# Matmuls of one array split grouped in a slot, tails loaded by batch, weights loaded later: a fused attention and channel-mix kernel

## The chip, the cores and the metric

The kernel runs on one core of one Trainium2 chip. The metric is the device time of one execution in microseconds (us), and medians of several executions are quoted. TensorE does the matmuls, VectorE and ScalarE work element by element, GpSimd casts and masks, and SyncE issues most DMA transfers. In the profile these are PE (its weight loads PEld), DVE, ACT, POOL and SP (SPq where issuing is meant). PEclk is the share of full speed that TensorE's clock was granted.

## The reference

Attention with a forget gate gives x, and a channel mix follows (the code is shortened). Batch is 8, heads 8, sequence 576, head size 64; the mix goes from 512 to 1024 features and back.

```python
def _attn_ref(q, k, v, f):
    scores = np.matmul(q, k.transpose(0, 1, 3, 2)) / np.sqrt(D)
    cum = np.cumsum(np.log(np.clip(f, 0.0001, 1.0)), axis=-1)
    decay = cum[:, :, :, None] - cum[:, :, None, :]
    scores = np.where(causal, -1e9, scores + decay)
    attn = np.exp(scores - np.max(scores, axis=-1, keepdims=True))
    attn = attn / (np.sum(attn, axis=-1, keepdims=True) + 1e-09)
    return np.matmul(attn, v)

def _moe_ref(x, mu_k, mu_r, w_k, w_v, w_r):
    x_prev = ...                              # x one token earlier, 0 first
    xk = mu_k * x + (1.0 - mu_k) * x_prev     # xr the same with mu_r
    k = np.maximum(xk @ w_k, 0.0)
    return (1.0 / (1.0 + np.exp(-(xr @ w_r)))) * (k * k @ w_v)
```

## The kernel before

Two heads of a batch are a pair; there are 32 pairs, four to a batch. The main loop goes through slots. In slot s the scores and exponentials of pair s are made in four pieces, q and k of pair s+1 are transposed (`tp`, then a copy to `qkT`), and the denominators of pair s-1 are summed. After a lag of 6 slots the numerators of pair s-6 (`values`) are multiplied by the reciprocals of their denominators, which gives `x`; `shift` makes `xk` and `xr` from it. Matmuls of the channel mix (`kp`, `rp`, `vp`) are kept in a queue, and `fill` takes some of them between the other steps. The loop, with loads, casts and the conditions for its ends cut:

```python
    LAG = 6
    for s in range(NP + LAG + 1):
        ...
        scores(s, 0); mask(s, 0)
        fill(gap)
        transposes(s + 1)
        fill(gap)
        scores(s, 1); mask(s, 1); mask(s, 2)
        fill(gap)
        denominators(s - 1)
        if s % PRW == 0:                  # PRW is 4, the pairs of a batch
            norm(s // PRW - 1)
        if s % PRW == LAG % PRW and s >= PRW + LAG:
            queue_mix((s - LAG) // PRW - 1)
        fill(gap)
        scores(s, 2)
        fill(gap)
        values(av, 0)                     # av = s - LAG
        fill(gap)
        scores(s, 3); mask(s, 3)
        fill(gap)
        values(av, 1)
        shift(av)
        fill(gap)
```

`norm` takes the reciprocals of a batch's denominators. They have to lie along the rows of a tile of 128 partitions, so they go out to DRAM (`scr`) and come back repeated over 64 partitions (`rb`), one tile to a pair:

```python
        scr = drp.tile([2, PRW, S], F32, name="scr")
        for half, o, n in ((0, 0, H0), (1, H0, S - H0)):       # H0 is 384
            for hh in range(2):
                r0 = 32 * (2 * half + hh)
                nc.sync.dma_start(out=scr[hh, :, o:o + n], in_=Rf[r0:r0 + PRW, 0:n])
        for p in range(PRW):
            rb = rbp.tile([P, S], F32, name="rb")
            for hh in range(2):
                nc.sync.dma_start(out=rb[hh * D:(hh + 1) * D, :],
                                  in_=scr[hh, p].unsqueeze(0).to_broadcast([D, S]))
            rbs[b * PRW + p] = rb
```

Scores use half of TensorE's rows, numerators half of its columns, denominators four columns, and everything else the full array. Each change from one to another costs about 0.10 us, as the prediction works out.

The softmax here doesn't subtract the row's maximum and nothing guards it: scores larger than these inputs give would overflow.

## Time and profile before

| Quantity | Before | Read from |
|---|---|---|
| Median time | 357.1 us (356.22 to 359.68, 4 runs) | runs beside the changed kernel |
| Span of the profiled run | 356.8 us | page |
| First score | 28.5 us | timeline |
| Slot 10 to slot 30, five batches | 84.80 to 267.40, 182.6 us | timeline, windows |

The slots 10 to 29 are five batches in the steady part. They are the best yardstick here, since each kernel does the same work in five such batches. The view by windows of the kernel before gives them so: stretch, its length, busy us and instructions of five engines, mean granted clock, DMA share, GB/s.

```profile
84.80:267.40 182.60, 177.71 (x1773) 94.81 (x1770) 136.72 (x252) 104.84 (x182) 95.59 (x140) 0.98 0.65 167
```

TensorE had no matmul open for 182.60 - 177.71 = 4.9 us of it, at a clock of 0.98.

### The profile page before, as it was taken

Reading aid. Unit: us, or ns where it says so; the run is one execution under the profiler, and the core shown is the slowest. Engines: PE = TensorE matmul, PEld = TensorE weight load, DVE = VectorE, ACT = ScalarE, POOL = GpSimd, SP = SyncE. Lnnn points to the kernel's source line nnn. Section 1 sums busy time; section 2 is a strip of 40 time slices with the busy share of each in tenths; the row PEclk is TensorE's granted clock in tenths of the full one; section 3 lists DMA queues with packets and bytes.
Section 4 is the critical chain, followed back from the end, with each engine's and each line's share of the span. In section 5 each row is a group of like instructions: output and inputs, shape, how many; then the busy total and the mean of one; then the engine's idle time right before and its main releaser. Section 6 shows DMA issues by size and latency. Waiting matters only on the chain.

```text
span 356.8 us, 7628 instructions
## 1 busy us (share of the span) xinstructions
PE 300.6 (84%) x2853; PEld 163.1 (46%) x2853; DVE 226.1 (63%) x443; ACT 175.6 (49%) x296; POOL 151.2 (42%) x231
## 2 busy tenths in 40 slices
PE   0006889577799999999999999999999978896995
PEld 0003445344445455545454555454545534553562
DVE  3043232397639786968697969685978677786442
ACT  1015667354637475647464756464646521440451
POOL 3003668577245574545555745355555322100000
PEclk9999999686989999999999999999999989999899
DMA  7996663764768576767754765676544315211012
GB/s 131 203 174 139 153 143 127 176 153 130 188 139 200 145 196 143 194 177 193 174 139 167 190 160 141 193 197 162 130 155 108 94 36 165 91 61 59 2 59 88
DMA packets 129029, 50.61 MB, mean 142 GB/s; under 512 B 118049, under 2 KB 119713, under 8 KB 128993
## 3 DMA queue, kind: packets, MB, share of 16 engines
q1 hardware_dynamic: 126896, 47.51, 52.1%
q0 software_dynamic: 2096, 2.62, 4.4%
q8 instruction: 22, 0.36, 0.4%
q14 instruction: 15, 0.11, 0.1%
HBM read 43.14 MB, written 9.58 MB: 148 GB/s over the span
## 4 chain that ended last, share of the span: by engine, by line
PE 53%; SPq 15%; DVE 13%; issue 5%; DMA 5%; ACT 4%; POOL 3%; POOLq 0%; DVEq 0%; ACTq 0%
PE vp L345 14%; PE kp L333 11%; SPq L96 9%; PE rp L345 7%; PE sc L226 6%; PE num L298 4%; PE tp L168 4%; DMA kf<-in_k_dram 4%; SPq L99 4%; PE den L259 3%; ACT a L232 3%; SPq L285 2%; PE vp L349 2%; DVE xk L322 2%; DVE x L304 2%
## 5 line engine op out<-in xcount | busy, mean ns | idle before, releaser
L232 ACT ACTIVATE a<-sc 128x1024 bf16<-128x1024 f32 (+2 forms) x128 | 105.8, 835 | 74.0 <-PE sc L226 70.1
L244 POOL TENSOR_SCALAR_AFFINE_SELECT a<-a 128x256 bf16<-128x256 bf16 (+2 forms) x128 | 62.1, 498 | 124.4 <-ACT a L232 119.8
L333 PE MATMUL kp<-xk,wk_sb 128*128 128x288 bf16 x512 | 76.7, 293 | 7.4 <-DVE xk L322 5.3
L337 ACT ACTIVATE rel<-kp 128x288 bf16<-128x288 f32 x128 | 51.6, 412 | 41.4 <-PE kp L333 27.7
L345 PE MATMUL vp<-wv_sb,relusq 128*128 128x512 bf16 x256 | 61.9, 385 | 2.0 <-DVE x L304 2.0
L333 PEld LDWEIGHTS <-wk_sb 128*128 128x128 bf16 x512 | 46.0, 99 | 26.9 <-issue 11.2
L226 PE MATMUL sc<-qkT 64*128 64x192 bf16 (+4 forms) x512 | 51.0, 282 | 7.8 <-ACT a L232 5.1
L158 POOL TENSOR_TENSOR vw<-vf,wbf 128x640 bf16<-128x640 f32 x32 | 45.5, 1423 | 20.2 <-PE num L298 11.8
L338 DVE TENSOR_TENSOR relusq<-rel 128x288 bf16<-128x288 bf16 x128 | 39.8, 331 | 18.9 <-ACT rel L337 17.6
L366 DVE SCALAR_TENSOR_TENSOR res<-th,vp 128x512 f32<-128x512 f32 x36 | 24.6, 683 | 37.7 <-PE vp L345 21.8
L304 DVE TENSOR_TENSOR x<-num,rb 128x384 bf16<-128x384 f32 x64 | 28.5, 456 | 20.8 <-PE num L298 18.6
L169 DVE COPY qkT<-tp 128x1152 bf16<-128x1152 bf16 x32 | 24.0, 750 | 26.1 <-PE tp L168 26.0
L226 PEld LDWEIGHTS <-qkT 64*128 64x128 bf16 x512 | 21.1, 100 | 42.3 <-issue 40.1
L322 DVE SCALAR_TENSOR_TENSOR xk<-diff,mu_k_sb,x 128x576 bf16<-128x576 bf16 x32 | 39.5, 1236 | 1.1
L359 ACT ACTIVATE th<-rp 128x512 f32<-128x512 f32 x36 | 21.5, 597 | 36.8 <-PE rp L345 33.4
L345 PEld LDWEIGHTS <-relusq 128*128 128x128 bf16 x256 | 23.7, 98 | 29.8 <-issue 3.2
L298 PE MATMUL num<-a,vw 128*64 128x192 bf16 (+4 forms) x512 | 36.3, 269 | 0.0
L345 PE MATMUL rp<-wr_sb,xr 128*128 128x512 bf16 x128 | 34.0, 389 | 0.0
L168 PE MATMUL tp<-ident,qb 128*128 128x128 bf16 (+1 forms) x160 | 19.3, 240 | 13.6 <-DVE qb L153 7.8
L322 DVE SCALAR_TENSOR_TENSOR xr<-diff,mu_r_sb,x 128x576 bf16<-128x576 bf16 x32 | 30.6, 956 | 0.0
L168 PE MATMUL tp<-ident,kb 128*128 128x128 bf16 (+1 forms) x160 | 19.4, 241 | 11.8 <-DVE kb L153 9.2
L298 PEld LDWEIGHTS <-vw 128*64 128x64 bf16 x512 | 22.0, 114 | 14.9 <-issue 11.1
(49 smaller groups left out, 186.7 us busy)
## 6 DMA issues: line engine op xcount, KB each, us to landing
rb<-scr SPq DMA_DIRECT2D x64, 144.0 KB
out_dram<-res SPq DMA_DIRECT2D x36, 256.0 KB
qf<-in_q_dram SPq DMA_DIRECT2D x64, 128.0 KB
kf<-in_k_dram SPq DMA_DIRECT2D x64, 128.0 KB
vf<-in_v_dram SPq DMA_DIRECT2D x64, 128.0 KB
wk_sb<-in_moe_w_k_dram POOLq DMA_DIRECT2D x1, 1024.0 KB, 9.7
qf<-in_q_dram SPq DMA_DIRECT2D x32, 32.0 KB
wv_sb<-in_moe_w_v_dram POOLq DMA_DIRECT2D x1, 1024.0 KB, 18.5
```

What stands on the lines that cost most here:

```text
L158: nc.gpsimd.tensor_tensor(out=vw[Pi % NV], in0=vf[Pi % NV], in1=wbf[:, :, 2 * Pi:2 * Pi + 2].unsqueeze(3).to_broadcast([P, NC, 2, D]), op= ...
L168: nc.tensor.transpose(tp[:, i, c * P:c * P + sz], src[:sz, c, :], ident[:sz, :sz])
L226: nc.tensor.matmul(sc[:, hh, col - off:col - off + n], lhsT=t[lo:lo + D, 1, kb * P:(kb + 1) * P], rhs=t[lo:lo + D, 0, q0:q0 + n], start=Tr ...
L232: nc.scalar.activation(out=a[:, :, off:off + w], in_=sc[:, :, 0:w], func=AF.Exp, scale=SCALE)
L244: nc.gpsimd.affine_select(out=v_, in_=v_, compare_op=ALU.is_ge, fill=0.0, base=0, pattern=pat, channel_multiplier=-1)
L298: nc.tensor.matmul(nm[hh * D:(hh + 1) * D, q0 - o:q0 - o + w], lhsT=t[:, kb, hh, :], rhs=a[:, hh, col:col + w], start=(kb == 0), stop=(kb ...
L304: nc.vector.tensor_tensor(out=xs[Pi % NX][:, 1 + o:1 + o + n], in0=nm[:, 0:n], in1=rbs[Pi][:, o:o + n], op=ALU.mult)
L322: nc.vector.scalar_tensor_tensor(out=dst[:, p, :], in0=diff, scalar=mu[:, p:p + 1], in1=x[:, 0:S], op0=ALU.mult, op1=ALU.add)
L333: nc.tensor.matmul(kp[:, :HB], lhsT=wk_sb[:, db, fb * P:(fb + 1) * P], rhs=xks[b][:, db, hf * HB:(hf + 1) * HB], start=(db == 0), stop=(db ...
L337: nc.scalar.activation(rel, kp[:, :HB], func=AF.Relu)
L338: nc.vector.tensor_mul(rsq[b][:, fb, hf * HB:(hf + 1) * HB], rel, rel)
L345: nc.tensor.matmul(ps, lhsT=tiles[b][:, i, t0:t0 + P], rhs=w[:, i, :], start=(i == 0), stop=(i == n - 1))
```

## The change

Its intent is to take away changes of the array's split (427 before, 185 after, counted in the built order) and to start earlier. It has five parts:

- Scores stand two and two, and the denominators together with both halves of the values, so that matmuls of one split follow each other. `fill` is called three times in a slot, and gates and values of the mix are queued half a batch later.
- The last 64 tokens (the tail) of q, k and v come once a batch, in one transfer each.
- The weights are loaded in slots 1 to 3 instead of at the start, q and k of the first pair come on two queues, and the casts of pair 1 stand behind the chain of f.
- The tails are transposed at full height, which spares two changes of the split for each tensor.
- The reciprocals of four pairs are one tile: one `scr` and four `rb` transfers instead of four and eight. The lag falls from 6 to 5, so the exponentials need six buffers instead of seven; the rows have two tiles of four pairs instead of six of one. `norm` moves to the end of its slot, and the values of the last three pairs come one or two slots earlier.

```diff
-        Rf = R.rearrange("p a b -> p (a b)")
-        scr = drp.tile([2, PRW, S], F32, name="scr")
+        scr = drp.tile([4, 32, H0], F32, name="scr")
+        nc.sync.dma_start(out=scr.rearrange("g r c -> (g r) c"),
+                          in_=R.rearrange("p a b -> p (a b)"))
+        rb = rbp.tile([P, PRW, S], F32, name="rb")
         for half, o, n in ((0, 0, H0), (1, H0, S - H0)):
             for hh in range(2):
-                r0 = 32 * (2 * half + hh)
-                nc.sync.dma_start(out=scr[hh, :, o:o + n], in_=Rf[r0:r0 + PRW, 0:n])
+                nc.sync.dma_start(
+                    out=rb[hh * D:(hh + 1) * D, :, o:o + n],
+                    in_=scr[2 * half + hh, 0:PRW, 0:n].unsqueeze(0).to_broadcast([D, PRW, n]))
 ...
-    LAG = 6
+    LAG = 5
 ...
         if live:
             scores(s, 0)
             mask(s, 0)
-        fill(gap)
 ...
             scores(s, 1)
             mask(s, 1)
             mask(s, 2)
+        fill(1.4)
+        if s + 1 < NP:
+            transposes(s + 1)
 ...
+        fill(1.2)
+        if live:
+            scores(s, 2)
+            scores(s, 3)
+            mask(s, 3)
 ...
         if 0 <= s - 1 < NP:
             denominators(s - 1)
-            if s % PRW == 0:
-                norm(s // PRW - 1)
+        for Pi in avs:
+            values(Pi, 0)
+            values(Pi, 1)
 ...
+        if 0 < s <= NP and s % PRW == 0:
+            norm(s // PRW - 1)
+        for Pi in avs:
 ...
+            shift(Pi)
+        fill(2.5)
```

Cut from this diff, mostly without a mark, are the loads, the tails, the weights, the queue of the mix and removed lines of the old loop.

## The prediction

> **What bounds the kernel now.** I read the page's busy shares and slices first, then the waits, then the timeline of single stretches, because TensorE is busy 84% of the span and an average hides where the other 16% lies. The slices (40 of 8.9 us; digits are tenths):
>
> ```profile
> PE 300.6 (84%) x2853; PEld 163.1 (46%) x2853; DVE 226.1 (63%) x443; ACT 175.6 (49%) x296; POOL 151.2 (42%) x231
> ...
> PE   0006889577799999999999999999999978896995
> ...
> PEclk9999999686989999999999999999999989999899
> DMA  7996663764768576767754765676544315211012
> ```
>
> There are three regimes. For three slices TensorE does nothing while DMA is full; up to slice 11 it has holes and a lowered clock; from then on it is full. In the full part its own stream sets the end. What that stream consists of is read from the timeline (start us, length us, engine, line, operation, count):
>
> ```profile
> 155.10 1.90 PE L345 MATMUL vp<-wv_sb,relusq 128*128 128x512 bf16 x8
> 156.94 0.34 PE L226 MATMUL sc<-qkT 64*128 64x192 bf16 x4
> ...
> 161.45 0.53 PE L168 MATMUL tp<-ident,qb 128*128 128x128 bf16 x5
> 161.91 0.53 PE L168 MATMUL tp<-ident,kb 128*128 128x128 bf16 x5
> ```
> ```profile
> 345.91 1.89 PE L345 MATMUL vp<-wv_sb,relusq 128*128 128x512 bf16 x8
> 347.64 1.03 PE L345 MATMUL rp<-wr_sb,xr 128*128 128x512 bf16 x4
> 348.50 1.89 PE L345 MATMUL vp<-wv_sb,relusq 128*128 128x512 bf16 x8
> ```
>
> The reader should compare starts. Eight vp matmuls before a rp of the same shape take 347.64 - 345.91 = 1.73 us, 216 ns each. The same eight before a sc, which uses half the rows, take 1.84 us. Changing the split of the array costs about 0.10 us. The five transposes confirm it: four at 56 ns and a half-width one at 27 ns are 0.25 us, yet 0.46 us pass, because the 64-row tail switches twice.
>
> The start is a chain of a load and of VectorE's order:
>
> ```profile
> 17.26 0.49 DVE L153 CAST kb<-kf 128x640 bf16<-128x640 f32 x1 [9.51 <-DMA kf<-in_k_dram]
> ...
> 24.64 0.39 DVE L182 TENSOR_SCALAR lf<-lf 64x576 f32<-64x576 f32 x1
> ...
> 28.25 0.55 PE L191 MATMUL wtp<-ident,wrow 64*128 64x64 f32 x3 [9.68 <-ACT wrow L187]
> ```
>
> The first k tile comes at 17.3 us, while 2.5 MB of weights share the DMA engines; the f chain waits behind the casts of pair 1. First score: 28.5 us. Later holes are those of the SyncE queue, which issues without a break:
>
> ```profile
> 62.70 1.09 SPq L96 DMA_DIRECT2D kf<-in_k_dram  x2
> 63.84 0.63 SPq L99 DMA_DIRECT2D kf<-in_k_dram  x1
> 64.56 1.10 SPq L96 DMA_DIRECT2D vf<-in_v_dram  x2
> 65.70 0.61 SPq L99 DMA_DIRECT2D vf<-in_v_dram  x1
> 66.36 1.14 SPq L96 DMA_DIRECT2D qf<-in_q_dram  x2
> ```
>
> One tensor of a pair costs 1.8 us of issuing, q, k and v 5.5 us a slot, against slots of 4.65 to 4.9 us at first. After the 5 us of eight rb issues slots 7, 8 and 9 (sc start to sc start) last 9.4, 6.2 and 7.0 us.
>
> **What the Trainium skill says.** "TensorEngine Tiling (Array Packing)", Tiling Modes, Key Properties: changing the tiling mode, not just the tile, drains TensorE. The trace agrees: 0.10 us. "TensorE: Matmul & The Clock Gate", Back-to-back issue gap, gives N/2.4 + 2.5 ns, so 216 ns at 512 columns; the trace has 216. "Trainium Kernel Development and Optimization", Key Constraints: DMAs of the SP, ACT and POOL queues share the same 16 engines, and a second issuing engine saves only issue time. Here the k loads on ScalarE therefore save issue time, and only the later weights free bandwidth. "SBUF — State Buffer", Who interferes with whom: VectorE operations can be blocked for the length of a GpSimd operation. The trace agrees: xk takes 1.70 us at 160.53 while vw runs from 160.16 to 161.62, and 0.82 us at its shortest.
>
> **The change part by part.** I counted the tile sizes in the built order: 427 switches before, 185 after. Per slot without switches, from the timeline's starts: scores 0.65, denominators 0.37, numerators 0.74, transposes 0.50 us (0.56 with full-height tails). A kp matmul takes 0.124 us, a vp or rp 0.2165 (the half-column ones go in pairs).
>
> - Base before: 32 x (0.65 + 0.37 + 0.74 + 0.50) = 72.3; 512 x 0.124 = 63.5; 432 x 0.2165 = 93.5; f transposes 0.5. Sum 229.8. Switches 427 x 0.098 = 41.8. Stream 271.6 us.
> - Base after: + 32 x 0.06 = 231.7. Switches 185 x 0.098 = 18.1. Stream 249.8 us. TensorE has 21.8 us less to do, if nothing stops it.
> - The start: q, k, two tails and f are 0.94 MB and, at the 170 to 200 GB/s of the first windows, 5 us on top of some 2 us before the first byte. So f is there at about 7 us. Casts, tail casts and ten transposes bring VectorE to 9.5, the f chain takes 4 us as it does now (24.6 to 28.5). First score at about 14 us, 14.5 earlier.
> - Early slots: two score groups now stand together with two score buffers shared with tp, so tp waits for the first exponential (1.02 us), the last scores wait for the qkT copy. With the slow clock: 0.65 to the exponential, to 1.7; tp to 2.85; copy 3.1 to 3.9; last scores 4.2; denominators 5.1. A slot is 5.2 us, with numerators (1.6 us slow) 6.8. Slots 0 to 8: 5 x 5.2 + 4 x 6.8 = 53, so slot 9 starts at 67 us. Issuing is no longer the limit: 3.4 us a slot and a quarter of three tails. The first kp waits for x, norm (2.1 us, 6 operations), diff and xk: 4 us more. First kp at 71 us; it is at 88 now.
> - VectorE: the qkT copy grows by 128/1152, 32 x 0.08 = 2.7 us. It stands just ahead of the last scores.
> - POOL's casts and vw lose a fifth, and get it back as tail work. It is not the bound.
>
> **The rest of the span.** Before its first kp the new kernel has done 23 us of stream, so 227 us remain. To that I add holes. The built order has no channel-mix work in slots 12, 16, 20, 24 and 28. In those a VectorE chain is bare: qkT copy behind the shift of the slot before, last scores, denominators, numerators, x, norm, diff, xk, first kp of the next batch. From numerators to xk that is 0.3 + 0.36 + 2.1 + 0.5 + 0.82 = 4.1 us, of which TensorE can fill 1.3; the lag of VectorE from the two slots before adds 2 to 5 us. I choose 6 us a batch, five times: 30. The rb rows now have one slot instead of two to arrive; norm's end to the last rb is 9.7 us now (186.4 to 196.1) with 12 issues, some 6 with 5: I put 1 us a batch, 5. Half-clock windows after the holes: 3. The end: 6 of holes against 7.5 now, since the last three pairs come earlier; 4 us from the last matmul to the end as now. 71 + 227 + 30 + 5 + 3 + 6 + 4 = **346 us**. The same sum for the kernel before closes: 88 + 245 + 20 of holes and low clock + 4 = 357.
>
> **The rivals.** (1) TensorE remains the bound all through: holes of 2 us a batch and the other terms as above. Then 71 + 227 + 10 + 3 + 2 + 5 + 4 = 322. For it speaks that VectorE is busy only 63%; against it that VectorE works in order and that the slots without mix bunch its norm and shifts. (2) VectorE takes the place of the switches: holes of 8 to 9 us a batch, as I get when xk takes 1.70 us in both slots ahead, and each hole brings the clock down. The start's gain of 17 us is then given back: 356 to 362. The PEclk row speaks for it, since holes of about 2 us were followed by half-clock windows. (3) DMA limits the head: by the first kp 61 us of engine time are needed (packet times of the trace summed over 16 engines, weights 15.7), so in 67 us it would be 91% busy. Weights in slots 1 to 3 then hold q and k back by 3 to 6 us: 350. The queue's round of packets and three buffers speak against more.
>
> **Range and chances.** The head's gain is the surest part (12 to 18 us). The stream's 22 us are sure too, but my trace by hand of the slots gives most of them back. A change that groups matmuls so deliberately was likely tuned to keep more, so I take 346 rather than rival 2, with 330 to 360. Under 350.5 us is faster by over 2%: 0.62. Between: 0.33. Over 364.8: 0.05.
>
> **What would show it.** First score near 14 us and first kp near 71; switches still at 0.10 us; slots with only scores, transposes, denominators and numerators with several us of TensorE idle, ended by VectorE (qkT, xk); waits of x on rb. I am wrong upward if those holes exceed 8 us or the early slots wait for q and k; wrong downward if VectorE keeps up, and then the time is near 322.

## More of the kernel before

VectorE was busy 137 us and had time for more. Its longest waits were on TensorE. The rows `rb` are not among them (engine, what it ran, releaser, us in total, times, longest):

```profile
DVE qkT L169 <- PE tp L168: 26.0, 10, 3.9
DVE res L366 <- PE vp L345: 21.8, 14, 2.4
DVE x L304 <- PE num L298: 18.6, 15, 2.1
```

## The result, and the profile after

The changed kernel is correct and slower: 395.94 us median (393.57 to 399.15, 4 runs) against 357.1. The ratio is 1.108 (95% interval 1.098 to 1.118). Ratios here are the mean time of one kernel's fast runs over the mean of the other's in the same rounds, so they are not quite the ratios of the medians quoted. The range of 330 to 360 us doesn't hold the result.

The page of the changed kernel begins so (the slices are 9.86 us long):

```profile
PE 298.9 (76%) x2826; PEld 181.0 (46%) x2853; DVE 225.1 (57%) x438; ACT 174.7 (44%) x296; POOL 159.3 (40%) x256
...
PE   1477544775967986799678987889678984699996
...
PEclk9999999789989998899969996899959996699999
DMA  9799899379458926794449644853646234220112
...
PE kp L355 10%; PE vp L367 10%; DMA rb<-scr 8%; PE rp L367 5%; DVE xk L344 5%; PE num L320 4%; DVE xr L344 3%; DVE diff L342 3%; ACT a L255 3%; DVE x L326 3%; DVE qkT L192 3%; PE den L282 2%; DMA scr<-R 2%; PE sc L249 2%; POOL a L267 2%
```

Where the kernel before has an unbroken row of nines for TensorE, this one has a dip in every batch, and the clock row has a 5 to 8 beside most of the later dips. (The nines at its start are no measurement: the first clock record of this trace is at 71.4 us, and the ten scores just before it, at 70.30, still take 1.04 us, where they take 0.61 at full clock.) VectorE and ScalarE are no busier than before, and GpSimd, which is no bound, has 8 us more. In the chain that ended last (the lowest line) a new member stands third: the rows `rb` on their way from DRAM. The view by windows says the same of the five batches, which are slots 9 to 28 here because the lag is one less, and of the rest:

```profile
76.13:286.62 210.49, 169.59 (x1731) 103.84 (x1746) 135.37 (x250) 104.27 (x180) 101.72 (x155) 0.92 0.65 142
...
286.60:394.40 107.80, 88.41 (x662) 50.20 (x668) 57.97 (x123) 37.23 (x76) 18.77 (x26) 0.89 0.29 81
```

The batches take 210.5 us instead of 182.6. TensorE is busy 8 us less, so the change did take work from it. But it has no matmul open for 210.49 - 169.59 = 40.9 us where it was 4.9, and its clock is 0.92 instead of 0.98. (Some 15 matmul records are missing from this stretch; by the gaps that nothing else explains, they make little over 1 us of the 40.9.) What it waits for is seen on VectorE, whose longest waits are now:

```profile
DVE x L326 <- DMA rb<-scr: 60.7, 16, 10.4
DVE relusq L360 <- ACT rel L359: 28.2, 45, 1.8
DVE qkT L192 <- PE tp L191: 21.1, 7, 4.1
```

Sixteen waits are two in each of the eight batches. One batch shows how they come about. First VectorE around slot 17, the first slot that needs the rows of batch 3:

```profile
158.11 0.37 DVE L296 STREAM_TRANSPOSE R<-rt 64x192 f32<-64x192 f32 x1
...
161.36 0.65 DVE L360 TENSOR_TENSOR relusq<-rel 128x288 bf16<-128x288 bf16 x2
167.58 0.56 DVE L326 TENSOR_TENSOR x<-num,rb 128x384 bf16<-128x384 f32 x1 [5.57 <-DMA rb<-scr]
169.42 0.36 DVE L326 TENSOR_TENSOR x<-num,rb 128x192 bf16<-128x192 f32 x1 [1.27 <-DMA rb<-scr]
169.69 0.52 DVE L360 TENSOR_TENSOR relusq<-rel 128x288 bf16<-128x288 bf16 x2
170.13 0.68 DVE L388 SCALAR_TENSOR_TENSOR res<-th,vp 128x512 f32<-128x512 f32 x1
```

Then the issues of SyncE in the same stretch of the changed kernel, and those of the kernel before in a like one (start, length, what is issued, count):

```profile
158.96 0.45 SPq L299 DMA_DIRECT2D scr<-R  x1
161.35 2.57 SPq L304 DMA_DIRECT2D rb<-scr  x4
163.96 1.15 SPq L99 DMA_DIRECT2D qf<-in_q_dram  x2
```
```profile
186.40 1.29 SPq L281 DMA_DIRECT2D scr<-R  x4
188.30 4.95 SPq L285 DMA_DIRECT2D rb<-scr  x8
```

The norm's last operation ends at 158.48, and the rows are first used at 167.58, 9.1 us later; the second half is used at 169.42, 10.9 us later. Issuing did become half as long, 2.57 instead of 4.95 us, but the bytes are the same 1.18 MB. The first two transfers carry the first halves of all four pairs (384 KB each, says the page), so the first pair has to wait for the others' rows too. It is so in every batch: from the second on, the last rows land 10.1 to 12.5 us after the norm's end. In the meantime VectorE does nothing of what stands behind the waiting `x` in its order: a `rel` that ScalarE finished at 165.9 is squared at 169.7. TensorE in the same stretch:

```profile
163.95 0.85 PE L320 MATMUL num<-a,vw 128*64 128x384 bf16 x14
164.64 0.20 PE L320 MATMUL num<-a,tail 128*64 128x64 bf16 x2
164.76 0.67 PE L355 MATMUL kp<-xk,wk_sb 128*128 128x288 bf16 x4
165.93 0.65 PE L355 MATMUL kp<-xk,wk_sb 128*128 128x288 bf16 x4 [0.50 <-ACT rel L359]
167.07 1.89 PE L367 MATMUL vp<-wv_sb,relusq 128*128 128x512 bf16 x7 [0.50 <-ACT rel L359]
168.80 0.65 PE L355 MATMUL kp<-xk,wk_sb 128*128 128x288 bf16 x4
169.95 0.65 PE L355 MATMUL kp<-xk,wk_sb 128*128 128x288 bf16 x4 [0.50 <-ACT rel L359]
```

Both numerator tiles are finished at 164.8 and wait for `x`. They hold two of the three PSUM buffers that numerators, `kp`, `rp` and `vp` share. So each group of four `kp` waits until ScalarE has emptied the one that is left: a group every 1.15 us, where four take 0.50 otherwise.

In the first batch it is worse, since the weights fill the DMA at that time and SyncE stands behind slow issues:

```profile
35.32 4.08 SPq L99 DMA_DIRECT2D vf<-in_v_dram  x2
39.50 4.05 SPq L99 DMA_DIRECT2D qf<-in_q_dram  x2
43.65 1.00 SPq L99 DMA_DIRECT2D kf<-in_k_dram  x2
44.70 2.16 SPq L99 DMA_DIRECT2D vf<-in_v_dram  x4
46.96 0.45 SPq L299 DMA_DIRECT2D scr<-R  x1
49.66 2.58 SPq L304 DMA_DIRECT2D rb<-scr  x4
```

The norm was done at 40.6. The rows were sent out at 47.0 and read back from 49.7, and `x` began at 55.8 after a wait of 10.4 us.

The lowered clock comes mostly from slots without channel-mix work: by the clock records of the trace, each of the seven half-clock stretches that begin in slots 10 to 28 begins in such a slot (12, 16, 20, 24, 28) or in the one after it (17, 21). In slots 16 and 28 of the changed kernel the single holes are 0.2 to 1.6 us; this is the end of slot 28 and the start of 29:

```profile
282.26 0.38 PE L191 MATMUL tp<-ident,qb 128*128 128x128 bf16 x4 [0.95 <-ACT a L255]
...
283.18 0.34 PE L249 MATMUL sc<-qkT 64*128 64x192 bf16 x4 [0.20 <-ACT a L255]
285.12 0.26 PE L249 MATMUL sc<-qkT 64*128 64x192 bf16 x2 [1.59 <-DVE qkT L192]
...
286.62 1.03 PE L249 MATMUL sc<-qkT 64*128 64x384 bf16 x10
```

The windows of 3.4 us in the same stretch, the first number after the length being TensorE's busy time and the third from the right the clock:

```profile
279.70:283.10 3.40, 2.33 (x50) 1.83 (x39) 2.66 (x5) 2.24 (x3) 3.01 (x5) 1.00 0.72 188
283.10:286.50 3.40, 1.73 (x38) 1.28 (x37) 2.14 (x4) 1.33 (x3) 2.50 (x5) 0.99 0.71 161
286.50:289.90 3.40, 2.65 (x28) 1.96 (x23) 3.26 (x9) 1.94 (x2) 3.40 (x6) 0.50 0.34 71
```

After the window with 1.73 us of work the clock is halved, and ten scores take 1.03 us instead of 0.61. By the trace, slot 17 above runs at half clock for 3.4 us too, from 160.2. The busy time of a window doesn't foretell this alone: the window 91.90:95.30 of the same trace has 1.58 us of matmul, and the clock stays full in it and after it. In the clock records of all 17 traces no window of 3.41 us with more than 2.07 us of matmul was followed by half clock; from 1.46 to 2.07 us both occur.

### The profile page after: what moved, and what is told of

It reads as the page before. It is cut to its first block, busy times and chain, and to the rows that moved or that the text cites. A ratio compares the mean times of both kernels' runs of the same rounds, so it can differ in the third digit from the quotient of the medians.

```text
span 394.4 us, 7397 instructions
## 1 busy us (share of the span) xinstructions
PE 298.9 (76%) x2826; PEld 181.0 (46%) x2853; DVE 225.1 (57%) x438; ACT 174.7 (44%) x296; POOL 159.3 (40%) x256
## 4 chain that ended last, share of the span: by engine, by line
PE 37%; DVE 24%; DMA 15%; POOL 9%; issue 5%; ACT 5%; SPq 3%; ACTq 0%; POOLq 0%; DVEq 0%
PE kp L355 10%; PE vp L367 10%; DMA rb<-scr 8%; PE rp L367 5%; DVE xk L344 5%; PE num L320 4%; DVE xr L344 3%; DVE diff L342 3%; ACT a L255 3%; DVE x L326 3%; DVE qkT L192 3%; PE den L282 2%; DMA scr<-R 2%; PE sc L249 2%; POOL a L267 2%
## 5 line engine op out<-in xcount | busy, mean ns | idle before, releaser
L255 ACT ACTIVATE a<-sc 128x1024 bf16<-128x1024 f32 (+2 forms) x128 | 102.0, 836 | 69.5 <-PE sc L249 69.4
L355 PE MATMUL kp<-xk,wk_sb 128*128 128x288 bf16 x512 | 82.3, 300 | 21.3 <-DVE xk L344 11.5
L326 DVE TENSOR_TENSOR x<-num,rb 128x384 bf16<-128x384 f32 x64 | 27.6, 458 | 82.2 <-DMA rb<-scr 60.7
L249 PE MATMUL sc<-qkT 64*128 64x192 bf16 (+4 forms) x512 | 47.2, 296 | 24.5 <-DVE qkT L192 21.8
L360 DVE TENSOR_TENSOR relusq<-rel 128x288 bf16<-128x288 bf16 x128 | 45.4, 380 | 28.7 <-ACT rel L359 28.2
L173 POOL TENSOR_TENSOR vw<-vf,wbf 128x512 bf16<-128x512 f32 x32 | 38.2, 1195 | 6.6 <-PE num L320 6.6
L320 PE MATMUL num<-a,vw 128*64 128x192 bf16 (+3 forms) x448 | 33.9, 300 | 7.5 <-DVE x L326 5.9
L192 DVE COPY qkT<-tp 128x1280 bf16<-128x1280 bf16 x32 | 26.1, 815 | 21.1 <-PE tp L191 21.1
L344 DVE SCALAR_TENSOR_TENSOR xk<-diff,mu_k_sb,x 128x576 bf16<-128x576 bf16 x32 | 33.6, 1049 | 1.1
L191 PE MATMUL tp<-ident,qb 128*128 128x128 bf16 x128 | 14.8, 249 | 23.4 <-ACT a L255 14.3
L320 PEld LDWEIGHTS <-vw 128*64 128x64 bf16 x448 | 22.9, 126 | 16.2 <-issue 10.2
L191 PEld LDWEIGHTS <-qb 128*128 128x128 bf16 x128 | 10.9, 108 | 28.6 <-issue 15.6
```

The lines of the kernel that those rows point to most:

```text
L173: nc.gpsimd.tensor_tensor(out=vw[Pi % NV], in0=vf[Pi % NV], in1=wbf[:, :4, 2 * Pi:2 * Pi + 2].unsqueeze(3).to_broadcast([P, 4, 2, D]), op= ...
L192: nc.vector.tensor_copy(qkT[Pi % NQK], tp[:, :, 0:640])
L249: nc.tensor.matmul(sc[:, hh, col - off:col - off + n], lhsT=t[lo:lo + D, 1, kb * P:(kb + 1) * P], rhs=t[lo:lo + D, 0, q0:q0 + n], start=Tr ...
L255: nc.scalar.activation(out=a[:, :, off:off + w], in_=sc[:, :, 0:w], func=AF.Exp, scale=SCALE)
L320: nc.tensor.matmul(nm[hh * D:(hh + 1) * D, q0 - o:q0 - o + w], lhsT=t[:, kb, hh, :] if kb < 4 else tl[:, 2 * p + hh, :], rhs=a[:, hh, col: ...
L326: nc.vector.tensor_tensor(out=xs[Pi % NX][:, 1 + o:1 + o + n], in0=nm[:, 0:n], in1=rbs[Pi][:, o:o + n], op=ALU.mult)
```

## The experiments

Fifteen kernels were run in three rounds each, with the kernel before beside them (medians of 357.5 to 358.2 us). The changed kernel was not run again beside them; its own rounds had the kernel before at 357.1. The profiled runs of the first two below were slow, as were three of the four runs of the second and one of a_valpair. The table has what all of them did in five batches, from the view by windows: slots 9 to 28 at lag 5 and 10 to 29 at lag 6. "Open" is the time without a matmul, length less TensorE's busy time.

| Run | Median us | Five batches us | Open us | Clock |
|---|---|---|---|---|
| before | 357.1 | 182.6 | 4.9 | 0.98 |
| after | 395.9 | 210.5 | 40.9 | 0.92 |
| a_stale (profile of a slow run) | 368.8 | 198.8 | 29.3 | 0.90 |
| a_lag6 (profile of a slow run) | 362.0 | 186.8 | 22.7 | 0.95 |
| a_norm_early | 388.9 | 206.5 | 32.8 | 0.90 |
| a_rbpair | 378.6 | 202.5 | 32.7 | 0.92 |
| a_early_pair | 369.8 | 199.2 | 29.3 | 0.92 |
| b_group6 | 371.4 | 186.2 | 21.3 | 0.97 |
| a_oldloop6 | 344.7 | 174.5 | 5.9 | 0.99 |
| a_lag6_oldq | 363.3 | 193.6 | 27.1 | 0.96 |
| a_scorepair | 352.6 | 187.0 | 15.7 | 0.96 |
| a_valpair | 342.4 | 173.6 | 8.5 | 1.00 |
| b_lag5 | 349.1 | 177.8 | 1.3 | 0.99 |
| a_oldloop5 | 343.0 | 176.0 | 6.3 | 0.99 |
| a_oldloop5_rbpair | 340.7 | 174.2 | 3.6 | 0.99 |
| b_start | 354.3 | 183.8 | 7.4 | 0.98 |
| b_full | 353.1 | 178.0 | 7.9 | 0.99 |

The theory after the result was that the late rows cost most of the loss. The rivals were that the grouped order itself does, or the slots without mix, or the new start.

### Do the rows' waits cost the time?

**a_stale** is the changed kernel, but each batch is multiplied by the rows of the batch before it, which have long arrived; a third buffer keeps them. Its output is wrong, which doesn't matter for the time.

```diff
-            rbs[b * PRW + p] = rb[:, p, :]
+            rbs[b * PRW + p] = (held[-1] if held else rb)[:, p, :]
+        held.append(rb)
```

> The changed kernel at lag five, but the values of a batch are multiplied with the reciprocal rows of the batch before (wrong result on purpose); all loads stay. Theory A: no wait on the rows of this batch, so the time falls as with the longer lag, 335 to 350 us. Theory C, the form of the row loads itself (rows of 1536 and 768 bytes, a scratch of 196 KB) hurts by holding up the other loads: the time stays above 370 us although x no longer waits.

Measured: 368.83 us, ratio 1.030 (1.022 to 1.038). Only the first batch still waits. So the waits cost some 27 of the 39 us, and the kernel without them is still 3% slower than the one before. The time lies between the two theories: the waits are the larger part of the loss, and there is a second part.

**a_lag6** gives the rows one slot more.

```diff
-    ap_ = ctx.enter_context(tc.tile_pool(name="attn", bufs=6))
+    ap_ = ctx.enter_context(tc.tile_pool(name="attn", bufs=7))
-    LAG = 5
+    LAG = 6
```

> The changed kernel with the values six slots behind the scores instead of five (and seven attention buffers), nothing else. Theory A, the reciprocal rows arrive too late because only one slot lies between norm and the first values: the waits of x on rb (60.7 us of VectorE in the changed kernel) fall under 8 us, slots 13, 17, 21, 25 lose 5 us or more, and the time falls to 335 to 350 us, below the kernel before. Theory B, VectorE's order and the two score buffers bind anyway and the rb wait only stands where TensorE would have waited too: 370 us or more. A value between means both.

Measured: 361.99 us (356.51 to 364.65). One of its four runs is fast, so there is no ratio; but its slowest run is 29 us below the fastest of the changed kernel. VectorE's wait on the rows falls from 60.7 to 7.2 us. The waits fell as theory A had it, but its 335 to 350 us were not reached. So the smaller lag, a part of the change that looked like a mere saving of buffers, stands behind most of the loss in this loop, and again something is left.

**a_norm_early** puts the norm ahead of the values in its slot.

```diff
+        if 0 < s <= NP and s % PRW == 0:
+            norm(s // PRW - 1)
         for Pi in avs:
             values(Pi, 0)
             values(Pi, 1)
 ...
-        if 0 < s <= NP and s % PRW == 0:
-            norm(s // PRW - 1)
```

> The changed kernel with norm put ahead of the values of its slot, where the kernel before has it relative to the denominators. It ends some 2 to 3 us earlier. Theory A: each batch gains about that, 8 x 2 to 3 us, so 370 to 380 us, and the waits on rb fall from 60.7 to some 40 us. Theory B: no gain, since x and shift of that slot come 2 us later: 390 us or more.

Measured: 388.88 us, ratio 1.087 (1.080 to 1.095). The waits on the rows are 35.7 us, as low as theory A had them, but only 7 us are gained: the time lies between both forecasts.

**a_rbpair** gives the changed kernel the norm's transfers of before: four to `scr`, then two a pair, 144 KB each by the page, with a tile for each pair (eight such tiles, the same space).

```diff
-        rb = rbp.tile([P, PRW, S], F32, name="rb")
 ...
+        for p in range(PRW):
+            rb = rbp.tile([P, S], F32, name="rb")
+            for hh in range(2):
+                nc.sync.dma_start(out=rb[hh * D:(hh + 1) * D, :],
+                                  in_=scr[hh, p].unsqueeze(0).to_broadcast([D, S]))
```

> The changed kernel (grouped, lag five) with the reciprocal rows loaded as in the kernel before: four small scratch writes and, pair by pair, eight loads of 147 KB into one tile a pair, so that the first x needs two loads and not all four pairs' rows. Theory C (form: the first x waits for 786 KB of rows of all four pairs): the waits on rb fall from 60.7 to 20 to 35 us and the time to 365 to 380 us. If the distance of one slot alone counts, the first pair comes hardly earlier and the time stays at 388 to 396 us.

Measured: 378.55 us, ratio 1.061 (1.055 to 1.067); waits on the rows 25.4 us. Both are as theory C had it. Twelve small transfers beat five large ones by 17 us; in them the first pair's rows come first. By the packets in its trace, from the second batch on, they land 5.0 to 6.6 us after the norm's end, and the last pair's 9.0 to 11.9.

**a_early_pair** does both at once.

> The changed kernel with its norm moved ahead of the values in its slot AND with the reciprocal rows loaded pair by pair (each alone gave 388.9 and 378.6 us against 396). Theory A, the rows' arrival is what the changed kernel waits for, and norm's late place and the all-four-pairs form are the two reasons why a lag of 5 is too short for it although the kernel before runs at 349 us with a lag of 5: VectorE's x then waits at most some 15 us in all on rb (as in the kernel before at lag 5; 60.7 in the changed kernel), and the time falls to 362 to 368 us, where the changed kernel at lag 6 stands. Rival, the two gains only add (7 and 17 us): 371 us, with 20 us or more of waits on rb left. Rival that they overlap: 376 us or more.

Measured: 369.76 us, ratio 1.035 (1.028 to 1.043). This is VectorE's wait on the rows in it, as the waits of its profile have it:

```profile
DVE x L326 <- DMA rb<-scr: 2.3, 2, 1.6
```

The waits are gone, more fully than expected, and the time is that of a_stale (368.8). Two independent ways of removing the waits agree: they cost 26 to 27 us. Of the 26 us here, 3.6 lie before slot 9, 11.3 in the five batches and 11.5 behind them (the stretches are 72.6, 199.2 and 96.3 us). The holes that go fit the reading of slot 17: in the five batches the matmuls of the mix waited 13.6 us for ScalarE's `rel` or for VectorE's `x`, the two that empty their buffers; here it is 4.5. The expected 362 to 368 us was too low; the single gains added up give 371. At lag 6 there are at least 8 us less still (most of a_lag6's runs were slow ones), which the rows' waits don't explain. A reading of the trace, not isolated by a run: at lag 5 the norm falls into the slot without mix, and those slots (12, 16, 20, 24, 28) are 6.5 us long on average in the changed kernel; at lag 6 (slots 13, 17, 21, 25, 29) they are 5.7.

### What does the grouping do by itself?

**b_group6** is the kernel before with the changed loop and queue alone, at lag 6 (278 changes of the split instead of 427).

> The kernel before with the changed kernel's loop and mix queue alone (scores in two groups, denominators and values together, late gate and value work), at lag six; loads, tails, weights and transposes as before. 278 switches instead of 427, so 14.6 us less of stream. Theory D: the holes of the slots without mix work eat that: 355 to 370 us, same or slower. Theory E: 340 to 347 us.

Measured: 371.36 us, ratio 1.037 (1.031 to 1.042). **a_oldloop6** is the reverse, the changed kernel with loop and queue of before, at lag 6 (335 changes; a_lag6 has 184). The edit of both is the exchange of the loop that the change section shows.

> The changed kernel's loads, tails, late weights, rb form and full-height transposes with the loop and the mix queue of the kernel before (scores, denominators and values apart, mix work in seven gaps a slot, lag six). 335 switches against 184 in a_lag6, so 14.8 us more of stream. Theory D, the grouping's bare slots and the half-clock windows after them cost more than its switches save: no slots with 2 us and more of idle after slot 12, and the time is 335 to 350 us, under a_lag6 (362). Theory E, the grouping gains and the loads or the rb form lose: 365 us or more.

Measured: 344.69 us, ratio 0.963 (0.958 to 0.968). So the grouped loop loses on either base: 13 us on the kernel before (358.2 beside it), and 17 us between a_oldloop6 and a_lag6 (12 with the one fast run of a_lag6), although TensorE has fewer changes of the split to make. Theory D held both times (b_group6 is 1 us above its range). The table shows where: the grouped loop leaves some 21 to 23 us without a matmul in five batches, the old one 5 to 6. On the kernel before this takes back a little more than the 12.8 us that TensorE is busy less (164.9 against 177.7): the five batches are 3.6 us longer, and the other 9.8 us of b_group6's span lie before slot 10 (88.9 instead of 84.8) and behind slot 30. What ends these holes is in the waits of the five batches; a_lag6 (a slow run) has

```profile
PE tp L191 <- ACT a L255: 9.2, 10, 1.0
PE sc L249 <- ACT a L255: 5.5, 10, 0.9
```

and b_group6 (a fast one) has 9.3 and 4.5 us. These are transposes and scores that wait for an exponential, mostly in the slot without mix and the one after it; the two score buffers serve both. In a_oldloop6 no transpose waits so in the five batches, and scores wait 2.0 us. The number of `fill` calls, three instead of seven in a slot, was not varied alone.

**a_lag6_oldq** keeps the grouped loop at lag 6, but queues the mix as before, so that no slot is without mix work.

```diff
             for t0 in blocks[hf]:
-                late.append((0.86, b, gate_unit, t0))
-                late.append((1.72, b, value_unit, t0))
+                todo.append((0.86, b, gate_unit, t0))
+                todo.append((1.72, b, value_unit, t0))
```

> a_lag6 (grouped scores, denominators and values together) with the mix queue of the kernel before, which spreads mix work over all slots: no slot without it; 190 switches. Theory D1, the loss of the grouping is the bare slots that the late queue leaves, with VectorE's norm and shift chain exposed in them: the time falls from 362 to 335 to 345 us, at or under a_oldloop6 (344.7), since 14 us of switches are saved. Theory D2, grouping as such loses (two score buffers, last scores behind the qkT copy, VectorE's shift after both values): 352 us or more.

Measured: 363.34 us, ratio 1.018 (1.012 to 1.025). That is no better than a_lag6, as theory D2 had it. The slots without mix aren't the cause by themselves: given mix work, the holes stay or move elsewhere (27.1 us without a matmul; of these, transposes wait 11.7 us for the exponential and `kp` 10.7 us for ScalarE).

**a_scorepair** starts from a_oldloop6 and groups only the scores (253 changes).

```diff
         scores(s, 0)
+        scores(s, 1)
         ...
         scores(s, 2)
+        scores(s, 3)
```

> The changed loads, tails, late weights and transposes with the loop of before at lag 6 (344.7 us, 335 changes of the array's split), but the scores grouped two and two: 253 changes, 8.0 us less stream. Theory G1, the scores' grouping is what loses (two score buffers: the transposes wait for the exponential, the second score group for the copy of qkT): 346 us or more, with more than 10 us of TensorE waits of tp on ACT. Theory G2, the bunching of denominators, values, x and shift at the slot's end loses instead, through VectorE's order: then this run keeps its 8 us and shows 336 to 339 us. If both lose in part: 340 to 345.

**a_valpair** starts from a_oldloop6 and puts only denominators and both halves of the values together, at the slot's end (273 changes).

```diff
         scores(s, 3)
+        denominators(s - 1)
+        norm(...)
+        values(av, 0)
         values(av, 1)
```

> The same loop of before at lag 6 (344.7 us), scores apart as before, but denominators and both halves of the values together at the slot's end: 273 changes of the split instead of 335, 6.1 us less stream. Theory G2 (the bunching at the slot's end loses, through VectorE's order): 346 us or more, with more relusq, xk and qkT waits in the slots without channel mix. Theory G1 (the scores' grouping loses): 338 to 340 us. If both lose in part: 341 to 345.

Measured: a_scorepair 352.60 us, ratio 0.988 (0.982 to 0.993); a_valpair 342.39, ratio 0.956 (0.950 to 0.963). The scores' grouping loses 8 us although it has 8.0 us less to do. Putting the values together gains 2 us of the 6.1 that its 62 changes fewer are worth, and a difference of 2 us is within the two runs' spread. The theory that the bunching at the slot's end loses falls. But it isn't as the other theory had it either: the transposes' wait on ScalarE in a_scorepair is 6.0 us, below the 10 us expected. These are its longest waits of TensorE in the whole span and, second, one slot's hole:

```profile
PE tp L191 <- POOL qb L163: 10.0, 5, 4.9
PE vp L367 <- DVE x L326: 8.3, 5, 1.7
PE tp L191 <- ACT a L255: 6.0, 8, 1.0
```
```profile
255.83 0.61 PE L249 MATMUL sc<-qkT 64*128 64x384 bf16 x10
258.11 1.89 PE L367 MATMUL vp<-wv_sb,relusq 128*128 128x512 bf16 x8 [1.66 <-DVE x L326]
```

Over the span the waits are spread over GpSimd's casts, VectorE's `x` (the release of a numerator's buffer) and ScalarE. In the five batches all 8.3 us of `vp` on `x` lie, over half of the 15.7 us there; a_oldloop6 has 2.5 us of this wait. Which of them would have to be shortened for grouped scores to pay was not tried and stays open.

### The lag, the rows and the start on the old loop

**b_lag5** is the kernel before with `LAG = 5` and nothing else.

> The kernel before with lag five instead of six, nothing else. There norm stands before the values in its slot and the last rows landed 9.7 us after norm. Theory A: waits of x on rb appear, of some 2 to 5 us a batch, and the time rises by 8 to 30 us, to 365 to 385 us. Theory B or C: within 2% of the kernel before or a little faster, since the pipeline is a slot shorter.

Measured: 349.06 us, ratio 0.976 (0.969 to 0.984). The interval lies across the border of 2%, but the loss that theory A had doesn't come. A lag of 5 does the old loop no harm, with its norm in the middle of the slot and rows by pair: the rows cost 14.8 us of VectorE's waits but no holes of TensorE in the five batches (1.3 us). Before them the span is 6.6 us shorter (slot 9 at 78.2 instead of slot 10 at 84.8).

**a_oldloop5** is a_oldloop6 with `LAG = 5`.

> The same with lag five. With the norm in the middle of its slot the rows need to land within a slot of some 9 us; the kernel before gained 8.5 us from lag five although x waited 14.8 us in all on rb. Theory D: 328 to 345 us, at or under a_oldloop6. If the single norm load of four transfers is later than the eight of the kernel before, waits of x on rb of 3 us and more a batch and 350 us or more.

Measured: 343.03 us, ratio 0.957 (0.951 to 0.964). The wait on the rows is large in it, and yet costs little:

```profile
DVE x L326 <- DMA rb<-scr: 28.4, 12, 9.2
```

TensorE has no matmul open for only 6.3 us in its five batches. So VectorE's wait on the rows is not a loss in itself. From the second batch on the rows land 10.9 to 12.8 us after the norm's end, as late as in the changed kernel, but the norm comes earlier in its slot: the waits in the five batches are 10.9 us here and 36.0 there. Taking 18 us of all waits away (the next run) gains only 2.3 us. The trace of slot 17 suggests why the grouped order pays more: both numerator tiles are held at once there, and the mix has one buffer left. No run isolates that.

**a_oldloop5_rbpair** adds the rows by pair.

> The changed loads, tails and full-height transposes in the loop of the kernel before at lag five, with the rows loaded pair by pair. In a_oldloop5 x waited 28.4 us on rb, most of it in the first two batches. Theory C: those waits fall to about 10 us and the time from 343.0 to 333 to 340 us. Otherwise 341 to 345 us.

Measured: 340.73 us (339.92 to 342.0), ratio 0.954 (0.949 to 0.960), correct. The waits on the rows are 10.6 us, as expected, but the gain on a_oldloop5 is 2.3 us, just short of theory C, and within the spread. (The waits of a_oldloop5 lie for less than half in the first two batches, 13.4 of 28.4 us, not for most.) It has the lowest median of all that were run, 4.6% under the kernel before, though not clear of a_valpair and a_oldloop5. It keeps the tails by batch, the late weights, the full-height transposes and the lag of 5, and drops the grouping and the large row transfers.

**b_start** is the kernel before with the changed start: weights in slots 1 to 3, the first k and f on ScalarE's queue, the cast of pair 1 after the f chain.

```diff
-    load_qk(0)
-    nc.sync.dma_start(out=lf, in_=f_bh[:, :])
+    load(q, qf[0], 0)
+    load(k, kf[0], 0, nc.scalar)
+    nc.scalar.dma_start(out=lf, in_=f_bh[:, :])
 ...
-    nc.gpsimd.dma_start(out=wk_sb, in_=moe_w_k.rearrange("(db p) ff -> p db ff", p=P))
 ...
+        if 1 <= s <= 3:
+            load_weights(s - 1)
```

> The kernel before with the changed start alone: weights in slots 1 to 3, k of pair 0 and f issued by ScalarE, the casts of pair 1 after the f chain. First score near 14 us instead of 28.5. If the early slots keep their length, the time falls by 12 to 15 us, to 342 to 346 us. If the displaced weights and the SyncE queue (5.5 us of issuing a slot) hold up q and k, slots 3 to 9 grow and less than 6 us are left: 351 us or more.

Measured: 354.30 us, ratio 0.988 (0.983 to 0.993). The first score comes at 13.0 instead of 28.5 us, and 4 us are left of these 15 at the end. Slot 10 begins 5.4 us earlier. GpSimd's casts now wait longer for q; in the kernel before it was 10.9 us in all:

```profile
POOL qb L155 <- DMA qf<-in_q_dram: 19.5, 3, 8.7
```

Only the first of these waits, 3.8 us up to 42.5, lies in the time of the weights, whose packets run from 22.6 to 41.7 us. The other two, at 61 and 92 us, come when those have long landed: before the second, SyncE issued the q transfer at 56.3, behind twelve issues of the norm.

**b_full** changes only the tails' transposes of the kernel before to full height.

```diff
-                sz = P if c < 4 else 64
-                nc.tensor.transpose(tp[:, i, c * P:c * P + sz], src[:sz, c, :], ident[:sz, :sz])
+                nc.tensor.transpose(tp[:, i, c * P:(c + 1) * P], src[:, c, :], ident)
```

> The kernel before with full-height tail transposes alone: 335 switches instead of 427, 92 x 0.098 = 9.0 us less, 64 half-width transposes made full-width, 1.7 us more. If TensorE's stream sets the end from slot 10 on: about two thirds of the 7.3 us lie in slots 10 to 31, so 5 to 7 us faster, 351 to 353 us. If the switch price is hidden: within 2 us of the kernel before.

Measured: 353.12 us, ratio 0.988 (0.982 to 0.993). There are 92 changes of the split fewer, 57 of them in five batches if they are spread evenly. An estimate from the prediction's price is 57 x 0.098 - 20 x 0.06 = 4.4 us for the five batches, with the higher tails taken off; they are 4.6 us shorter. That agrees, for one profiled run of each. Over the whole span the same estimate is 92 x 0.098 - 32 x 0.06 = 7.1, and 4.4 us came (353.1 beside 357.5).

## Why the prediction was wrong

- **The switches** were right. The order of matmuls in the traces gives the counts 427 and 185 too, the five batches of b_full agree with the price of 0.10 us, and TensorE's busy time fell by 8.1 us in five batches, by 12.8 in b_group6.
- **First score and early slots.** The first score is at 13.7 us, where the prediction has about 14; slots 0 to 4 take 4.93 us each against 5.2. Then it fails: slots 5 to 8 take 9.6, 13.2, 9.2 and 5.8 us, where 6.8 was put. Slot 9 begins at 76.1 us instead of 67, and the first `kp` at 78.9 instead of 71. Some 3.6 us of this are the rows (slot 9 begins at 72.6 in a_early_pair). For the rest, the trace shows delayed q: GpSimd's cast of q waits 8.2 us on the DMA, in two slots. The first wait, 3.1 us, ends at 41.7, when the weights have just landed, as rival 3 had it; the second, 5.1 us, is for a transfer that SyncE issued behind the rows.
- **The step that failed is the rows' term:** "norm's end to the last rb is 9.7 us now (186.4 to 196.1) with 12 issues, some 6 with 5: I put 1 us a batch, 5." It took the time from norm to rows to be one of issuing. Measured, the last rows come 10.1 to 12.5 us after the norm with 5 issues, no earlier than with 12. The wait is 60.7 / 8 = 7.6 us a batch, and removing it gains 26 to 27 us (a_stale, a_early_pair). The prediction also missed that all four pairs' rows come before the first can be used; a_rbpair shows this at 17 us.
- **The holes of VectorE's chain**, 6 us in each batch, were right in size in part by luck. With the rows' waits gone, a_early_pair has 29.3 / 5 = 5.9 us a batch without a matmul. But VectorE (`qkT`, `xk`) ends only 14.8 of these 29.3 us; the transposes' wait for the exponential, which the prediction had in the early slots alone, takes 8.7, and `kp` on ScalarE 3.5. In the changed kernel itself it is 40.9 / 5 = 8.2.
- **The half clock** was put at 3 us. Over the five batches the clock is 0.92, and 0.89 over the rest. If TensorE had had work all the time, that would be 210.5 x 0.08 + 107.8 x 0.11 = 29 us, an upper estimate. a_early_pair, without the waits, has 0.92 too, so this term was wrong also for the holes that were foreseen.
- **The sum.** The prediction's slot 9 (67), five batches and the rest can be split the same way. A batch is 249.8 / 8 = 31.2 us of stream, 6 of holes, 1 of rows and 0.6 of clock, together 38.8, so 346 is 67 + 194 + 85. The span shows 76.1 + 210.5 + 107.8 = 394.4. The miss is 9 us ahead of the batches, 16.5 in them, and 23 behind them, where the waits of the last two batches' rows and half-clock windows stand (TensorE has no matmul open for 107.80 - 88.41 = 19.4 us there). Without the rows' waits (a_early_pair) 72.6 + 199.2 + 96.3 = 368 us are left, so 6, 5 and 11 us of the miss come from elsewhere; for the last 11 the record shows no single cause.
- **The rivals.** Rival 2 named the direction, holes that eat what the switches save and bring the clock down. Without the rows' waits it would have been near: 362 to 370 us in a_lag6, a_stale and a_early_pair against its 356 to 362. The trust that a deliberate grouping "was likely tuned to keep more" had nothing from the profile behind it.

## What to carry to other kernels

Fewer transfers are not earlier data: ask which bytes the first consumer needs, and let them come first. What a wait of an in-order engine costs depends on the work and the buffers that stand behind it: rows as late after the norm cost 2 us or so in the loop that spreads its steps (a_oldloop5), where norm came earlier in its slot, and some 27 us in the one that bunches them. How much of that is the loop and how much the norm's place was not isolated. Before saving switches of a busy engine, check what the work between them was hiding. A lag can be shortened only after the slowest item that must arrive within it has been followed from its producer to its use.

## What the Trainium skill lacked or had wrong

- "TensorE: Matmul & The Clock Gate", Why this matters for your kernels, advises no idle gap of TensorE over about 3 us, lest the clock be halved. Here no single hole of slot 28 was over 1.59 us, and the clock was halved all the same for the stretch that followed. The same page's section on a second failure mode does say that frequent short idles between groups of matmuls make the clock swing; it gives no busy share at which that begins. In the 17 traces here the clock fell to half only after windows with at most 2.07 us of matmul in 3.41. The length of 3.4 us of such a window, which the page also gives, agrees: the half-clock stretches of the five batches last 3.4, 6.8 or 10.2 us.
- "DMA: Bandwidth & Descriptors", Rules for kernel authors, advises to coalesce small transfers into one large one. It doesn't say that a consumer then waits for bytes that it doesn't need ("Perfetto Trace Analysis", DMA Optimizations, comes nearer: smaller chunks may let some start sooner). Loads of 384 and 192 KB for four pairs instead of 144 KB for each half of a pair cut the issuing from 4.95 to 2.57 us and cost 17 us of the kernel's time (a_rbpair against the changed kernel).
- "TensorEngine Tiling (Array Packing)", Key Properties, says that a change of mode drains TensorE, without a duration. It was about 0.10 us here; 92 changes fewer in the kernel, some 57 of them in the five batches, made these 4.6 us shorter (b_full).
